# Sigmoid attention and a GELU feed-forward: weight and g tiles at their own places mod 64 bytes, and two blocks whose first products are issued in other forms

## The chip, the cores and the metric

One core of a Trainium2 chip runs the whole program. The metric is the device time of an execution in microseconds; the kernel before took 1192.64 us, the median of two runs (1191.70 and 1193.59). Its profiled execution took 1189.64 us.

## The reference

Attention with a sigmoid in place of the softmax, on 8 batches of 12 heads, 448 positions and 64 elements a head; then a feed-forward over the 3,584 tokens, of width 768 with 2,048 hidden units.

```python
scores = scale * np.matmul(q, k.transpose(0, 1, 3, 2)) - np.log(S)
attn = 1.0 / (1.0 + np.exp(-scores))
attn_out = np.matmul(attn, v)                       # 8 x 12 x 448 x 64
x = attn_out.transpose(0, 2, 1, 3).reshape(B * S, H * D)      # 3584 x 768
h = x @ w_in                                        # 3584 x 2048
g = 0.5 * h * (1.0 + erf(h / sqrt(2)))
out = g @ w_out                                     # 3584 x 768
```

The feed-forward's weights come as 64-bit floats.

## The kernel before

Attention runs first, in 24 steps of four heads each; its result x is parked in DRAM, with the model's 768 rows as 6 groups of 128 partitions and the tokens along the free dimension. Meanwhile a decoder on VectorE and ScalarE (lines 90 to 129) turns the 64-bit weights into 32-bit ones, reading every second word of `raw`, and writes them to DRAM too.

The feed-forward takes the tokens in 7 blocks of T = 512 (`t` from 0 to 6). Each block is two products. To keep precision, each operand is the sum of two rounded tiles, hi and lo (type float32r), and each product is three matmuls: lo weights by hi data, hi weights by lo data, hi weights by hi data.

- `ffn1(t)`, first product: for each of 16 units `fc` of 128 hidden rows, 6 groups `cc` of x times 3 matmuls go into one PSUM tile `ph` of 128 x 512 (lines 370 to 372). The moving operand is `xh[:, cc]` or `xl[:, cc]`, 512 words side by side. ScalarE then applies GELU twice, once to a float32 tile `gf` and once to the rounded `g` tile's first half, and VectorE subtracts the two to make the second half (lines 375 to 377).
- `ffn2(t, g)`, second product: for each of 6 groups `e` of output rows, 16 units times 3 matmuls go into `po` (lines 398 to 400); ScalarE copies `po` out, and SP's queue stores it.

So each product of a block is 288 matmuls, each with its own load of 128 x 128 weights. PSUM has four tiles for `ph` and `po` in turn.

`Weights` is what feeds the weights: `get(key)` is called as a unit begins, and `prepare_to(i + 4)` makes the units up to three ahead ready: a load from DRAM into one of three `wst` buffers (SP's queue), ScalarE's rounding to the hi part (line 184) and VectorE's subtraction for the lo part (line 185), into one of WHL = 4 `whl` buffers. The order of each engine's work is the order in which the program is written; a buffer that is asked for again waits for all who read it.

All tiles of the feed-forward have lengths that are multiples of 64 bytes, and all operands of its matmuls start a multiple of 64 bytes from their tile's start.

Of the kernel before, what the change touches and what calls it, by code (L numbers as in the profile page):

```python
# [8 lines left out]
F32 = mybir.dt.float32  # L9
F32R = mybir.dt.float32r  # L10
# [3 lines left out]
AF = mybir.ActivationFunctionType  # L14
ALU = mybir.AluOpType

P = 128
# [4 lines left out]
def tile_sigmoid_attention_gelu_ffn(  # L22
# [10 lines left out]
    nc = tc.nc  # L33
    B, NPAIR, _, S = q.shape
    NU = NPAIR // 2
    D = HALF
    NF, _, NC, _ = w_in.shape
    NO, _, NFH, _ = w_out.shape
# [3 lines left out]
    T = 512  # L42
# [5 lines left out]
    def psum(name, bufs):  # L48
        return tc.tile_pool(name=name, bufs=bufs, space=bass.MemoryType.PSUM)

    const = ctx.enter_context(tc.tile_pool(name="const", bufs=1))
    sb = ctx.enter_context(tc.tile_pool(name="sb", bufs=1))
# [3 lines left out]
    xh = const.tile([P, NPAIR, T], F32R, name="xh")  # L56
    xl = const.tile([P, NPAIR, T], F32R, name="xl")
# [4 lines left out]
    WU = max(NC, NFH) * P  # L62
    SUB_IN, SUB_OUT = NC * P, NFH * P // 2
    SUB = max(SUB_IN, SUB_OUT)
    WHL, WST = 4, 3
# [8 lines left out]
    def width(kind):  # L74
        return (NC if kind == "in" else NFH) * P
# [80 lines left out]
    dec = Decoder()  # L156
    AHEAD = 20

    class Weights:
# [17 lines left out]
        def prepare_to(self, n):  # L177
            while self.ready < min(n, len(self.units)):
                i = self.ready
                self.load_to(i + 1)  # L180
                t = self.staged.pop(i)
                w = width(self.units[i][1])
                hl = sb.tile([P, 2, WU], F32R, tag="whl", name=f"whl{i}", bufs=WHL)
                nc.scalar.copy(hl[:, 0, :w], t[:, :w])  # L184
                nc.vector.tensor_tensor(hl[:, 1, :w], t[:, :w], hl[:, 0, :w], op=ALU.subtract)  # L185
                self.split[i] = hl
                self.ready += 1
                self.load_to(i + WST)
# [6 lines left out]
    W = Weights()  # L195
# [4 lines left out]
    def load_x(t):  # L200
        nc.sync.dma_start(xl.bitcast(F32), scr_x[:, :, t * T : (t + 1) * T])

    def split_x():
        half = NPAIR // 2
        for h in slice(0, half), slice(half, NPAIR):
            nc.scalar.copy(xh[:, h], xl[:, h].bitcast(F32))
            nc.vector.tensor_tensor(xl[:, h], xl[:, h].bitcast(F32), xh[:, h], op=ALU.subtract)
# [151 lines left out]
                W.prepare_to(2)  # L359

    def feed_forward(ff, ps_f):
        def ffn1(t):
            g = []
            for fc in range(NF):
                ph = ps_f.tile([P, T], F32, tag="pf", name=f"ph{t}_{fc}")
                hl = W.get((t, "in", fc))
                for cc in range(NC):
                    wh = hl[:, 0, cc * P : (cc + 1) * P]
                    wl = hl[:, 1, cc * P : (cc + 1) * P]
                    nc.tensor.matmul(ph, wl, xh[:, cc], start=cc == 0, stop=False)  # L370
                    nc.tensor.matmul(ph, wh, xl[:, cc], start=False, stop=False)  # L371
                    nc.tensor.matmul(ph, wh, xh[:, cc], start=False, stop=cc == NC - 1)  # L372
                gt = ff.tile([P, 2, T], F32R, tag=f"g{fc}", name=f"g{t}_{fc}")
                gf = ff.tile([P, T], F32, tag="tmp", name=f"gf{t}_{fc}", bufs=3)
                nc.scalar.activation(gf, ph, AF.Gelu)  # L375
                nc.scalar.activation(gt[:, 0], ph, AF.Gelu)  # L376
                nc.vector.tensor_tensor(gt[:, 1], gf, gt[:, 0], op=ALU.subtract)  # L377
                g.append(gt)
                if t == 0:
                    dec.to(AHEAD + 10 * (fc + 1) / NF)  # L380
            return g

        def ffn2(t, g):
            for e in range(NE):
                po = ps_f.tile([P, T], F32, tag="pf", name=f"po{t}_{e}")
                for half in range(2):
                    hl = W.get((t, "out", 2 * e + half))
                    if t == 0:
                        dec.to(AHEAD + 10 + 2 * e + half + 1)
                    if e == 1 and half == 0 and t + 1 < NT:  # L390
                        load_x(t + 1)
                    if e == 2 and half == 0 and t + 1 < NT:
                        split_x()
                    for f in range(NFH):
                        fc = half * NFH + f
                        wh = hl[:, 0, f * P : (f + 1) * P]
                        wl = hl[:, 1, f * P : (f + 1) * P]
                        nc.tensor.matmul(po, wl, g[fc][:, 0], start=fc == 0, stop=False)  # L398
                        nc.tensor.matmul(po, wh, g[fc][:, 1], start=False, stop=False)  # L399
                        nc.tensor.matmul(po, wh, g[fc][:, 0], start=False, stop=fc == NF - 1)  # L400
                ob = ff.tile([P, T], F32, tag="tmp", name=f"ob{t}_{e}", bufs=3)
                nc.scalar.copy(ob, po)  # L402
                nc.sync.dma_start(out[e * P : (e + 1) * P, t * T : (t + 1) * T], ob)

        for t in range(NT):
            ffn2(t, ffn1(t))
# [6 lines left out]
    ff = ctx.enter_context(tc.tile_pool(name="ff", bufs=1))  # L413
    ps_f = ctx.enter_context(psum("ps_f", 4))
    feed_forward(ff, ps_f)


# [31 lines left out]
```

## Time and profile before

| | |
|---|---|
| median of the runs | 1192.64 us |
| profiled execution | 1189.64 us |
| its span, first to last instruction | 1187.9 us |
| TensorE busy, matmuls | 1170.8 us, 5,856 |
| granted TensorE clock | 0.999 |
| ScalarE, VectorE busy | 547.5 us, 528.1 us |
| GpSimd busy | 36.0 us |
| DMA, mean | 164 GB/s |

Attention takes about the first 267 us of the span, and the feed-forward's seven blocks the rest. In the rows of a profile an engine's time is busy time, PE is TensorE with its matmuls, PEld its weight loads, DVE VectorE, ACT ScalarE, and SPq the queue that issues DMAs. A matmul's duration includes the time until its last result is written, so matmuls that follow each other overlap in the rows; the distance from start to start is what one costs in a stream.

### The profile page before, as it was taken

What the parts mean: (1) busy time and instruction counts of PE and PEld (TensorE: products, weight loads), DVE (VectorE), ACT (ScalarE), POOL (GpSimd) and SP (SyncE); (2) the same over time, 40 slices, a digit from 0 to 9 for tenths busy, and PEclk for the clock granted to TensorE, in tenths of its full rate; (3) what the DMA queues carried; (4) which work ended last, traced back from release to release, by engine and by line L of the source; (5) the groups of instructions that cost most, each with busy time, mean ns of one, the idle gap of its engine ahead of it and who ended that gap; (6) DMA issues with size and microseconds to landing.
All of it is one profiled execution on the core that took longest, in us unless ns stands there. A gap on an engine that the chain in (4) does not pass through costs nothing.

```text
span 1187.9 us, 14649 instructions
## 1 busy us (share of the span) xinstructions
PE 1170.8 (99%) x5856; PEld 884.8 (74%) x5856; DVE 528.1 (44%) x643; ACT 547.5 (46%) x751; POOL 36.0 (3%) x56
## 2 busy tenths in 40 slices
PE   6999999999999999999999999999999999999998
PEld 3554544548888788888888888888888888888887
DVE  4777776447878334323432243324432343323420
ACT  6777777666644344324432343324432443324420
POOL 0111111000000000000000000000000000000000
PEclk9999999999999999999999999999999999999999
DMA  9999988646767533523343333433343334433330
GB/s 304 304 286 295 293 281 257 203 159 214 237 244 262 182 94 124 181 81 109 118 171 98 107 111 115 155 119 94 120 159 111 102 106 169 120 98 98 120 115 27
DMA packets 71300, 194.42 MB, mean 164 GB/s; under 512 B 6976, under 2 KB 19648, under 8 KB 71232
## 3 DMA queue, kind: packets, MB, share of 16 engines
q1 hardware_dynamic: 65536, 169.89, 45.6%
q0 software_dynamic: 5696, 23.60, 4.9%
q8 instruction: 46, 0.75, 0.3%
q14 instruction: 22, 0.18, 0.0%
HBM read 158.86 MB, written 34.60 MB: 163 GB/s over the span
## 4 chain that ended last, share of the span: by engine, by line
PE 81%; issue 15%; DMA 2%; POOL 1%; SPq 0%; ACT 0%; DVE 0%; POOLq 0%; ACTq 0%
PE po L398 11%; PE po L399 11%; PE po L400 11%; PE ph L370 11%; PE ph L371 11%; PE ph L372 11%; PE pav L298 7%; PE sc L264 5%; DMA qk<-k_dram 1%; PE sc_t L277 1%; PE pav L311 1%; POOL scr_out L128 0%; POOL scr_x L327 0%; DMA wst<-scr_out 0%; DMA scr_out<-wd_out 0%
## 5 line engine op out<-in xcount | busy, mean ns | idle before, releaser
L185 DVE TENSOR_TENSOR whl<-wst,whl 128x768 fp32r<-128x768 f32 (+1 forms) x196 | 210.0, 1072 | 299.3 <-ACT whl L184 296.5
L398 PE MATMUL po<-g,whl 128*128 128x512 f32 x672 | 261.8, 390 | 2.5 <-DVE whl L185 2.4
L370 PE MATMUL ph<-xh,whl 128*128 128x512 f32 x672 | 261.5, 389 | 0.0
L400 PE MATMUL po<-g,whl 128*128 128x512 f32 x672 | 261.4, 389 | 0.0
L399 PE MATMUL po<-g,whl 128*128 128x512 f32 x672 | 261.4, 389 | 0.0
L372 PE MATMUL ph<-xh,whl 128*128 128x512 f32 x672 | 261.4, 389 | 0.0
L371 PE MATMUL ph<-xl,whl 128*128 128x512 f32 x672 | 261.4, 389 | 0.0
L184 ACT CAST whl<-wst 128x768 fp32r<-128x768 f32 (+1 forms) x196 | 181.7, 928 | 140.5 <-PE po L400 117.2
L377 DVE TENSOR_TENSOR g<-gf,g 128x512 fp32r<-128x512 f32 x112 | 77.4, 692 | 232.0 <-ACT g L376 231.9
L375 ACT ACTIVATE gf<-ph 128x512 f32<-128x512 f32 x112 | 67.0, 598 | 224.4 <-PE ph L372 196.9
L252 ACT ACTIVATE a<-sc 128x896 f32<-128x896 f32 x144 | 121.9, 919 | 59.9 <-PE sc L264 59.9
L398 PEld LDWEIGHTS po<-g,whl 128*128 128x128 f32 x672 | 126.1, 188 | 29.9 <-DVE whl L185 3.8
L370 PEld LDWEIGHTS ph<-xh,whl 128*128 128x128 f32 x672 | 126.1, 188 | 26.9 <-DVE whl L185 0.7
L372 PEld LDWEIGHTS ph<-xh,whl 128*128 128x128 f32 x672 | 126.1, 188 | 26.3
L400 PEld LDWEIGHTS po<-g,whl 128*128 128x128 f32 x672 | 126.1, 188 | 26.3
L399 PEld LDWEIGHTS po<-g,whl 128*128 128x128 f32 x672 | 126.1, 188 | 26.1
L371 PEld LDWEIGHTS ph<-xl,whl 128*128 128x128 f32 x672 | 126.1, 188 | 26.1
L298 PE MATMUL pav<-a,v 128*64 128x448 f32 x576 | 118.6, 547 | 0.0
L402 ACT COPY ob<-po 128x512 f32<-128x512 f32 x42 | 24.7, 587 | 172.5 <-PE po L400 170.9
L298 PEld LDWEIGHTS pav<-a,v 128*64 128x64 f32 x576 | 37.2, 136 | 69.7 <-issue 69.7
L376 ACT ACTIVATE g<-ph 128x512 fp32r<-128x512 f32 x112 | 66.4, 593 | 0.0
L264 PE MATMUL sc<-lo,hi 64*128 64x448 f32 x288 | 58.4, 402 | 6.8 <-DVE lo L248 6.8
(35 smaller groups left out, 666.5 us busy)
## 6 DMA issues: line engine op xcount, KB each, us to landing
wst<-scr_in SPq DMA_DIRECT2D x112, 384.0 KB, 3.2
wst<-scr_out SPq DMA_DIRECT2D x84, 512.0 KB, 3.4
v<-v_dram SPq DMA_DIRECT2D x24, 512.0 KB, 5.2
raw<-w_in_dram SPq DMA_DIRECT2D x16, 768.0 KB, 8.0
raw<-w_out_dram SPq DMA_DIRECT2D x24, 512.0 KB, 5.1
scr_x<-x POOLq DMA_DIRECT2D x24, 448.0 KB, 6.8
xl<-scr_x SPq DMA_DIRECT2D x7, 1536.0 KB, 8.0
out_dram<-ob SPq DMA_DIRECT2D x42, 256.0 KB, 2.1
```

The source lines that it names most:

```text
L184: nc.scalar.copy(hl[:, 0, :w], t[:, :w])
L185: nc.vector.tensor_tensor(hl[:, 1, :w], t[:, :w], hl[:, 0, :w], op=ALU.subtract)
L252: nc.scalar.activation(a, sc, AF.Sigmoid, bias=NEG_LOG_S, scale=SCALE)
L264: nc.tensor.matmul(sc[:, j], ks[rows(j), 1, keys], qs[rows(j), 0], start=n == 0, stop=n == 2)
L298: nc.tensor.matmul(pav[rows(j)], vals[u][:, p, j, c], a[:, j], start=p == 0 and c == 0, stop=p == 1 and c == FULL - 1,)
L370: nc.tensor.matmul(ph, wl, xh[:, cc], start=cc == 0, stop=False)
L371: nc.tensor.matmul(ph, wh, xl[:, cc], start=False, stop=False)
L372: nc.tensor.matmul(ph, wh, xh[:, cc], start=False, stop=cc == NC - 1)
L377: nc.vector.tensor_tensor(gt[:, 1], gf, gt[:, 0], op=ALU.subtract)
L398: nc.tensor.matmul(po, wl, g[fc][:, 0], start=fc == 0, stop=False)
L399: nc.tensor.matmul(po, wh, g[fc][:, 1], start=False, stop=False)
L400: nc.tensor.matmul(po, wh, g[fc][:, 0], start=False, stop=fc == NF - 1)
```

## The change

It has five parts. `whl` and `g` tiles become 16 words longer, each under a name and buffer of its own. The data in a `whl` buffer starts 0, 4, 8 or 12 words into it, by buffer; that of `g` starts `fc` words in, 0 to 15. All blocks get this.

In block 1, units 0 to 11 take the moving operand x in another order of the 512 tokens: as rows of an `a` x `b` matrix read by columns, with `a` = lap = 2 (units 0 to 3), 32 (4 to 7) and 256 (8 to 11). Neighbours in the stream lie 256, 16 and 2 words apart. The results land in PSUM in stream order, and the two GELUs read them back with a step of lap words, so that `g` is in token order again. Units 12 to 15 of block 1 issue each matmul as two of 256 tokens.

In block 2, units 0 to 7 go two by two: for each `cc` and term, the matmul of one unit and then that of the other, into two PSUM tiles. Units 8 to 15 take the three terms in the order hi by lo, hi by hi, lo by hi.

```diff
@@ -180,7 +180,9 @@
                 self.load_to(i + 1)
                 t = self.staged.pop(i)
                 w = width(self.units[i][1])
-                hl = sb.tile([P, 2, WU], F32R, tag="whl", name=f"whl{i}", bufs=WHL)
+                hl = sb.tile([P, 2 * WU + 16], F32R, tag=f"whl{i % WHL}", name=f"whl{i}", bufs=1)
+                skip = 4 * (i % WHL)
+                hl = hl[:, skip : skip + 2 * WU].rearrange("p (x n) -> p x n", x=2)
                 nc.scalar.copy(hl[:, 0, :w], t[:, :w])
                 nc.vector.tensor_tensor(hl[:, 1, :w], t[:, :w], hl[:, 0, :w], op=ALU.subtract)
                 self.split[i] = hl
@@ -359,25 +361,62 @@
                 W.prepare_to(2)
 
     def feed_forward(ff, ps_f):
+        def whole(m):
+            return [(slice(0, P), m, slice(0, T))]
+
+        def shuffled(a):
+            return lambda m: [(slice(0, P), m.rearrange("p (a b) -> p b a", a=a), slice(0, T))]
+
+        def halves(m):
+            return [(slice(0, P), m[:, i : i + T // 2], slice(i, i + T // 2)) for i in (0, T // 2)]
+
+        def form(t, fc):
+            if t == 1 and fc < 12:
+                lap = (2, 32, 256)[fc // 4]
+                return shuffled(lap), lap
+            return (halves if t == 1 else whole), 1
+
+        def hidden(t, fcs):
+            phs = [ps_f.tile([P, T], F32, tag="pf", name=f"ph{t}_{fc}") for fc in fcs]
+            hls = [W.get((t, "in", fc)) for fc in fcs]
+            late = t == 2 and fcs[0] >= NF // 2
+            order = ((0, xl), (0, xh), (1, xh)) if late else ((1, xh), (0, xl), (0, xh))
+            split_to, lap = form(t, fcs[0])
+            for cc in range(NC):
+                for n, (x, m) in enumerate(order):
+                    for ph, hl in zip(phs, hls):
+                        w = hl[:, x, cc * P : (cc + 1) * P]
+                        for c, mv, ts in split_to(m[:, cc]):
+                            o = ph[c, ts]
+                            if lap > 1:
+                                o = o.rearrange("p (b a) -> p b a", a=lap)
+                            nc.tensor.matmul(
+                                o,
+                                w[:, c],
+                                mv,
+                                start=cc == 0 and n == 0 and ts.start == 0,
+                                stop=cc == NC - 1 and n == 2 and ts.stop == T,
+                            )
+            return [ph.rearrange("p (b a) -> p a b", a=lap) for ph in phs], {"a": lap}
+
         def ffn1(t):
             g = []
-            for fc in range(NF):
-                ph = ps_f.tile([P, T], F32, tag="pf", name=f"ph{t}_{fc}")
-                hl = W.get((t, "in", fc))
-                for cc in range(NC):
-                    wh = hl[:, 0, cc * P : (cc + 1) * P]
-                    wl = hl[:, 1, cc * P : (cc + 1) * P]
-                    nc.tensor.matmul(ph, wl, xh[:, cc], start=cc == 0, stop=False)
-                    nc.tensor.matmul(ph, wh, xl[:, cc], start=False, stop=False)
-                    nc.tensor.matmul(ph, wh, xh[:, cc], start=False, stop=cc == NC - 1)
-                gt = ff.tile([P, 2, T], F32R, tag=f"g{fc}", name=f"g{t}_{fc}")
-                gf = ff.tile([P, T], F32, tag="tmp", name=f"gf{t}_{fc}", bufs=3)
-                nc.scalar.activation(gf, ph, AF.Gelu)
-                nc.scalar.activation(gt[:, 0], ph, AF.Gelu)
-                nc.vector.tensor_tensor(gt[:, 1], gf, gt[:, 0], op=ALU.subtract)
-                g.append(gt)
+            f0 = 0
+            while f0 < NF:
+                fcs = range(f0, f0 + (2 if t == 2 and f0 < NF // 2 else 1))
+                phs, like = hidden(t, fcs)
+                for fc, ph in zip(fcs, phs):
+                    gt = ff.tile([P, 2 * T + 16], F32R, tag=f"g{fc}", name=f"g{t}_{fc}", bufs=1)
+                    gt = gt[:, fc : fc + 2 * T].rearrange("p (x n) -> p x n", x=2)
+                    gf = ff.tile([P, T], F32, tag="tmp", name=f"gf{t}_{fc}", bufs=3)
+                    gv, gh = (y.rearrange("p (a b) -> p a b", **like) for y in (gf, gt[:, 0]))
+                    nc.scalar.activation(gv, ph, AF.Gelu)
+                    nc.scalar.activation(gh, ph, AF.Gelu)
+                    nc.vector.tensor_tensor(gt[:, 1], gf, gt[:, 0], op=ALU.subtract)
+                    g.append(gt)
+                f0 = fcs[-1] + 1
                 if t == 0:
-                    dec.to(AHEAD + 10 * (fc + 1) / NF)
+                    dec.to(AHEAD + 10 * f0 / NF)
             return g
 
         def ffn2(t, g):
```

TensorE's order where block 1's unit 12 begins, before (line, operation, output<-inputs, size; `ph1_12` is the PSUM tile of block 1's unit 12, and the numbers behind names are those of buffers):

```order
L370 MATMUL ph1_12_4091<-xh_64,whl40_4005 128x512
L371 MATMUL ph1_12_4091<-xl_65,whl40_4005 128x512
L372 MATMUL ph1_12_4091<-xh_64,whl40_4005 128x512
L370 MATMUL ph1_12_4091<-xh_64,whl40_4005 128x512
L371 MATMUL ph1_12_4091<-xl_65,whl40_4005 128x512
L372 MATMUL ph1_12_4091<-xh_64,whl40_4005 128x512
```

and after, where `x2` and `x4` count rows alike that follow each other:

```order
L393 MATMUL ph1_12_4091<-xh_64,whl40_4005 128x256 x2
L393 MATMUL ph1_12_4091<-xl_65,whl40_4005 128x256 x2
L393 MATMUL ph1_12_4091<-xh_64,whl40_4005 128x256 x4
L393 MATMUL ph1_12_4091<-xl_65,whl40_4005 128x256 x2
L393 MATMUL ph1_12_4091<-xh_64,whl40_4005 128x256 x4
```

Each matmul of 512 columns has become two of 256, one behind the other; the terms follow as before. The units with a lap read like those of before in this listing, since it gives sizes and no steps.

ScalarE's order where block 2 begins, before (`whl59` is the weight unit 59, block 2's unit 3; `gf2_0` and `g2_0` are the GELUs of its unit 0):

```order
L402 COPY ob1_5_4581<-po1_5_4522 128x512
L184 CAST whl59_4585<-wst59_4526 128x768
L375 ACTIVATE gf2_0_4609<-ph2_0_4584 128x512
L376 ACTIVATE g2_0_4608<-ph2_0_4584 128x512
L184 CAST whl60_4614<-wst60_4555 128x768
L375 ACTIVATE gf2_1_4638<-ph2_1_4613 128x512
L376 ACTIVATE g2_1_4637<-ph2_1_4613 128x512
L184 CAST whl61_4643<-wst61_4588 128x768
```

and after:

```order
L441 COPY ob1_5_4653<-po1_5_4594 128x512
L186 CAST whl59_4658<-wst59_4598 128x768
L186 CAST whl60_4663<-wst60_4627 128x768
L413 ACTIVATE gf2_0_4705<-ph2_0_4656 128x512
L414 ACTIVATE g2_0_4704<-ph2_0_4656 128x512
L413 ACTIVATE gf2_1_4710<-ph2_1_4657 128x512
L414 ACTIVATE g2_1_4709<-ph2_1_4657 128x512
L186 CAST whl61_4716<-wst61_4661 128x768
L186 CAST whl62_4721<-wst62_4666 128x768
```

The cast of unit 60 has moved ahead of the first pair's GELUs. Its buffer is that of unit 56, which this pair's matmuls still read.

## The prediction

> **What bounds the kernel now.** I read the page's totals first, then the chain of waits, then the feed-forward in windows by stage, and last single matmuls in the timeline.
>
> ```profile
> span 1187.9 us, 14649 instructions
> PE 1170.8 (99%) x5856; PEld 884.8 (74%) x5856; DVE 528.1 (44%) x643; ACT 547.5 (46%) x751; POOL 36.0 (3%) x56
> PEclk9999999999999999999999999999999999999999
> PE 81%; issue 15%; DMA 2%; POOL 1%; SPq 0%; ACT 0%; DVE 0%; POOLq 0%; ACTq 0%
> PE po L398 <- DVE whl L185: 2.4, 2, 1.7
> ```
>
> TensorE is busy for 99% of the span at full granted clock, the chain that ends last is made of its matmuls, and over the whole feed-forward the matmuls of L398 waited 2.4 us for prepared weights. So an edit counts if it changes how far apart the matmuls start, or makes one of them wait. A window per stage shows the distance. The rows are the first product (ffn1) and the second (ffn2) of block 1, then ffn1 of block 2; the columns are window, length, and busy time with counts of PE, PEld, DVE, ACT, POOL.
>
> ```profile
> 400.76:466.04 65.28, 65.28 (x290) 54.05 (x289) 26.51 (x31) 29.09 (x47) 0.00 (x0) 1.00 0.36 111
> 466.04:531.32 65.28, 65.28 (x290) 54.05 (x289) 18.02 (x15) 18.13 (x21) 0.00 (x0) 1.00 0.41 131
> 531.32:596.60 65.28, 65.28 (x290) 54.05 (x289) 26.52 (x31) 29.07 (x47) 0.00 (x0) 1.00 0.34 111
> ```
>
> Each product is 16 x 18 = 288 matmuls (the counts take in two at the edges): 65.28 / 288 = 226.7 ns from start to start, in both products alike. Single rows say the same, and that each matmul's own weight load (PEld) starts with the matmul before it and so lies under it:
>
> ```profile
> 449.94 0.39 PE L371 MATMUL ph<-xl,whl 128*128 128x512 f32 x1
> 449.95 0.19 PEld L372 LDWEIGHTS ph<-xh,whl 128*128 128x128 f32 x1
> 450.17 0.39 PE L372 MATMUL ph<-xh,whl 128*128 128x512 f32 x1
> 450.17 0.19 PEld L370 LDWEIGHTS ph<-xh,whl 128*128 128x128 f32 x1
> 450.40 0.39 PE L370 MATMUL ph<-xh,whl 128*128 128x512 f32 x1
> ```
>
> Of the 226.7 ns, how much goes with the columns? The scores have 448 columns instead of 512 and come in pairs on two halves of the array:
>
> ```profile
> 61.43 0.19 PEld L264 LDWEIGHTS sc<-lo,hi 64*128 64x128 f32 x2 [0.70 <-ACT me L113]
> 61.54 0.19 PEld L264 LDWEIGHTS sc<-hi,lo 64*128 64x128 f32 x2
> 61.74 0.36 PE L264 MATMUL sc<-hi,lo 64*128 64x448 f32 x2
> 61.94 0.37 PE L264 MATMUL sc<-hi 64*128 64x448 f32 x2
> ```
>
> They stand 0.20 us apart, 0.027 less for 64 columns fewer: 0.42 ns a column, and so 226.7 - 512 x 0.417 = 13 ns that every matmul pays whatever its width. The two loads at the top, with nothing before them, start 0.11 us apart; that is how fast loads can follow each other.
>
> **The change part by part.**
>
> *Strided x (block 1, 12 of 16 units, 216 matmuls).* The moving operand's elements are taken 256 words apart (lap 2), 16 apart (lap 32) and 2 apart (lap 256), 72 matmuls each. PSUM is still written in order. No matmul of the trace reads with a step, so the price needs bounds. Below it is nothing: 226.7 ns stays. For what a matmul costs when each column takes twice as long to come, the nearest row is the probability times value product, which streams plain 32-bit floats at the same granted clock (the same run of matmuls, its first 4 and its first 6, that is one pair of 448 columns more):
>
> ```profile
> 63.45 0.97 PE L298 MATMUL pav<-a,v 128*64 128x448 f32 x4
> 63.45 1.35 PE L298 MATMUL pav<-a,v 128*64 128x448 f32 x6
> ```
>
> 0.38 us for 448 columns is 0.85 ns a column, 434 ns for 512, and 207 ns over the present spacing. Which laps pay it? One row of the trace reads SBUF with a step, the weight decoder, which takes every second word of `raw`; beside it a VectorE cast of contiguous data:
>
> ```profile
> L100 DVE TENSOR_SCALAR me<-raw 128x512 uint32<-128x512 uint32 x24 | 10.1, 421 | 0.0
> L100 DVE TENSOR_SCALAR me<-raw 128x768 uint32<-128x768 uint32 x16 | 9.0, 562 | 0.0
> L247 DVE CAST hi<-qk 128x896 fp32r<-128x896 f32 x24 | 15.2, 633 | 0.4 <-DMA qk<-k_dram 0.4
> ```
>
> 256 elements more cost 141 ns, 0.55 ns each, and at that slope 896 would take 421 + 384 x 0.55 = 632 ns, which is what the contiguous cast takes. A step of two words costs VectorE nothing. I take that for lap 256, and the doubled stream for laps 2 and 32, where no two neighbours in the stream are near each other in memory: 144 x 207 = 29.8 us. The ends are 0 and all three laps doubled, 216 x 207 = 44.7 us; a dearer case is a rival. That the far steps pay at all is my choice, and the weakest point here.
>
> The Trainium skill's page "SBUF — State Buffer", in section "Door 1: The DMA port swizzle", says that SBUF is read in lines of 16 bytes and that two hits on a line are needed for full bandwidth. By that rule lap 256 (two words of each line) is free and the other two pay; it gives no price, and the decoder's row agrees with it for the step of two.
>
> *Halves (block 1, last 4 units).* 72 matmuls become 144 of 256 columns, each with its own weight load. By the columns' slope a half takes 256 x 0.417 + 13 = 120 ns, over the 0.11 us in which loads can follow each other, so loads stay covered and a pair costs 240 for 227: 72 x 13 = 1.0 us. If the loads didn't fit, a half couldn't cost more than a whole does now: 72 x 227 = 16.3 us at most. From below, nothing: no row shows a matmul without the 13 ns.
>
> *Two by two, and the other order (block 2).* 288 matmuls of the same shape, each with its load: 0. Before, too, hi weights are loaded twice in a row (L371, L372), and each load has its own row. What moves is on ScalarE and VectorE:
>
> ```profile
> L375 ACT ACTIVATE gf<-ph 128x512 f32<-128x512 f32 x112 | 67.0, 598 | 224.4 <-PE ph L372 196.9 <-issue 27.6
> L376 ACT ACTIVATE g<-ph 128x512 fp32r<-128x512 f32 x112 | 66.4, 593 | 0.0
> L184 ACT CAST whl<-wst 128x768 fp32r<-128x768 f32 x112 | 93.4, 836 | 52.6 <-PE po L400 40.1 <-DMA wst<-scr_in 12.5
> L185 DVE TENSOR_TENSOR whl<-wst,whl 128x768 fp32r<-128x768 f32 x112 | 107.2, 957 | 98.3 <-ACT whl L184 96.2
> ```
>
> A pair asks for the weights four units on, whose buffer is that of the pair's first unit, so this cast now waits for the pair's own matmuls, and the pair's four gelus queue behind it on ScalarE. After a pair ends ScalarE runs cast, four gelus, cast: 0.84 + 2 x (0.60 + 0.59) + 0.84 = 4.1 us, and with VectorE's 0.96 the second weight of the pair after next is ready 5.0 us on. TensorE needs it after one more pair, 36 x 0.227 = 8.2 us. Cover left: 3.2 us. The gelus have emptied the pair's two PSUM buffers 3.2 us after its end, against the same 8.2. VectorE's queue (subtraction of weights, then two of g) follows within it, and the loads on SP's queue stand as far ahead as before. If the cover went, each of four pairs would lose what is over.
>
> *Gelu with a step in PSUM (block 1).* ScalarE is busy 29.09 of 65.28 us in this stage, by the window above. Were all 24 gelus twice as long, 24 x 0.6 = 14 us more still fit. 0.
>
> *Places mod 64 bytes.* Every one of the 4,032 feed-forward matmuls has another place for its weights, and those of ffn2 for g too (one word further per unit). No row shows an operand off a multiple of 64 bytes. From below: the 13 ns goes everywhere, -4,032 x 13 = -52 us. From above: the eight g tiles on odd words stream like the probabilities, 1,008 x 207 = +209 us. In each tile the words still follow each other, as they do in all contiguous rows, so I take 0 and keep both ends as rivals.
>
> **Sum**: 29.8 + 1.0 = 30.8 us. The profiled execution took 1189.64 us, 1.7 over its span; it becomes 1220.4. The median before is 1192.64, 3.0 above that execution, so the forecast is 1223.4, and its own range goes from 1222 (halves at nothing) to 1239 (halves at their most).
>
> **The rivals.** 2% of 1192.64 is 24 us, about what a measurement of this kernel can tell from no change.
>
> 1. *The step is free.* TensorE takes 32-bit words from any place at 0.44 ns each. For it: the step of two words is free on VectorE, and no row shows a stall by an address. Against it: the fixed 13 ns and the slower 0.85 ns rows show a stream that isn't far from some limit. Time: 1192.6 + 1.0 = 1193.6; ends not slower. It decides if laps 2 and 32 together cost under 23 us, 160 ns a matmul.
> 2. *All three laps double*: 44.7 + 1.0, 1238.3. For it: any step breaks a pair of neighbours; against it, the decoder's row.
> 3. *The read unit holds four words.* With one word used of it, a column takes four times 0.417: 853 + 13 = 866 ns, 640 over the present. Laps 2 and 32 then cost 92.2, lap 256 (two words of four, doubled) 14.9, halves 1.0: 1300.7. If lap 2, which goes back and forth between two places, keeps both units at hand, 46.1 less: 1254.6. For it: 4 bytes in 0.42 ns is the fastest stream of any row here (VectorE's is 0.55 ns, ScalarE's 128x768 cast 1.09), so spare reads are unlikely. Against it: nothing in the trace measures such a step.
>  The Trainium skill's "Vector Engine (DVE) Microarchitecture Reference", section "Measured stream behaviour on trn2", has 1.73 ns a column against 1.054 when one VectorE source hops every element, and the full rate for a source that alternates between two regions. An estimate from that page, 512 x 1.73 = 886 ns, would put the far laps beside rival 3, with lap 2 free or not; no run here shows it yet.
> 4. *One lap alone pays* (the 64-byte step, say): 14.9 + 1.0, 1208.5, within 2%.
> 5. *The places help.* The 13 ns is weight loads and streams that meet because all tiles start on the same 64 bytes; apart, they don't. With the step free it gives 1193.6 - 52 = 1141; with the forecast's laps 1171. For it: the 13 ns is there in every row, with a load under each matmul. Against it: it is the same to 0.1 ns in stages with other operands.
> 6. *Odd words hurt*: the 209 us above, about 1400 or more.
>
> **How the numbers follow.** Forecast 0.26; rival 1, 0.24; rival 2, 0.17; rival 3, 0.20 (0.11 for 1301, 0.09 for 1255); rival 4, 0.07; rival 5, 0.04; rival 6, 0.02. Slower by over 2%: 0.26 + 0.17 + 0.20 + 0.02 = 0.65. Within 2%: 0.24 + 0.07 = 0.31. Faster: 0.04. The range reaches from 1190.5 (rival 1 with halves at nothing and the runs' own spread) to 1260 (rival 3 with lap 2 free): it leaves out 1301, rivals 5 and 6, 0.17 in all.
>
> **What would show it.** In the profile after, ffn1 of block 1 should last 65.3 + 30.8 = 96 us, with matmuls 434 ns apart in its first eight units, 227 in the next four, and 120 in the halves; ffn1 of block 2 and every ffn2 should last 65.28, with no wait of TensorE for weights in block 2. The forecast is wrong if the first four or the second four units keep 227 ns or go past 434, if the third four leave 227, or if the window of any other block has another length than 65.28 us: then the places mod 64 bytes matter.

## The result, and the profile after

The changed kernel takes 1240.16 us, the median of two runs (1239.88 and 1240.45), against 1192.64: 47.5 us more, a ratio of 1.0403 with a 95% interval of 1.0382 to 1.0424. It is slower, as forecast, by half as much again as the 30.8 us of the sum, and inside the range.

The page's span, totals, clock and chain, after, and then the row of TensorE's waits for weights:

```profile
span 1238.1 us, 14800 instructions
PE 1220.5 (99%) x5928; PEld 893.9 (72%) x5928; DVE 528.0 (43%) x643; ACT 547.2 (44%) x751; POOL 36.2 (3%) x56
PEclk8999999999999999999999999999999999999999
PE 82%; issue 14%; DMA 2%; POOL 1%; SPq 0%; ACT 0%; DVE 0%; POOLq 0%; ACTq 0%
```

```profile
PE po L437 <- DVE whl L187: 1.3, 2, 1.1
```

TensorE is as full as before and waits no longer for weights (1.3 us against 2.4), so the time went into the spacing of matmuls. Windows by form show where. The first four rows are block 1's first product: laps 2, 32 and 256 with 72 matmuls each, then the halves with 144. The next two are block 2's first and second product, the last is block 3's first product, which has no form of its own, only the new places.

```profile
404.60:420.13 15.53, 15.53 (x73) 13.61 (x72) 5.92 (x7) 6.73 (x11) 0.00 (x0) 1.00 0.39 126
420.13:451.32 31.19, 31.19 (x74) 14.81 (x72) 6.61 (x8) 7.23 (x12) 0.00 (x0) 1.00 0.20 63
451.32:483.95 32.63, 32.63 (x73) 14.97 (x72) 6.61 (x8) 7.23 (x12) 0.00 (x0) 1.00 0.18 57
483.95:501.20 17.25, 17.25 (x145) 17.24 (x144) 7.41 (x8) 7.87 (x12) 0.00 (x0) 1.00 0.28 93
568.23:634.60 66.37, 66.37 (x289) 54.08 (x288) 26.55 (x31) 28.70 (x47) 0.00 (x0) 1.00 0.35 109
634.60:701.59 66.99, 66.99 (x289) 54.35 (x288) 18.02 (x15) 18.11 (x21) 0.00 (x0) 1.00 0.39 128
701.59:767.79 66.20, 66.20 (x289) 54.06 (x288) 26.54 (x31) 29.10 (x47) 0.00 (x0) 1.00 0.35 110
```

Before, 72 matmuls took 72 x 226.7 ns = 16.32 us, and each product 65.28 us. So:

| | us now | us before | per matmul | difference |
|---|---|---|---|---|
| lap 2 | 15.53 | 16.32 | 216 ns | -0.8 |
| lap 32 | 31.19 | 16.32 | 433 ns | +14.9 |
| lap 256 | 32.63 | 16.32 | 453 ns | +16.3 |
| halves | 17.25 | 16.32 | 120 ns a half | +0.9 |
| a plain first product | 66.20 | 65.28 | 230 ns | +0.9 each |
| block 2's first product | 66.37 | 65.28 | 230 ns | +1.1 |
| a second product | 66.99 | 65.28 | 233 ns | +1.7 each |

Block 1's forms cost 31.3 us together, near the sum of the prediction, but not by its terms: lap 2 is *faster* than neighbouring words, and lap 256, taken as free, is the dearest. The rest is in every block, and so belongs to the places.

### The profile page after: what moved, and what is told of

The parts are those of the page before. It is cut to its first block, busy times and chain, and to the rows that moved or that the text cites. A ratio compares the mean times of both kernels' runs of the same rounds, so it can differ in the third digit from the quotient of the medians.

```text
span 1238.1 us, 14800 instructions
## 1 busy us (share of the span) xinstructions
PE 1220.5 (99%) x5928; PEld 893.9 (72%) x5928; DVE 528.0 (43%) x643; ACT 547.2 (44%) x751; POOL 36.2 (3%) x56
## 4 chain that ended last, share of the span: by engine, by line
PE 82%; issue 14%; DMA 2%; POOL 1%; SPq 0%; ACT 0%; DVE 0%; POOLq 0%; ACTq 0%
PE ph L393 35%; PE po L437 11%; PE po L439 11%; PE po L438 11%; PE pav L300 6%; PE sc L266 5%; DMA qk<-k_dram 2%; PE sc_t L279 1%; PE pav L313 1%; POOL scr_out L128 0%; POOL scr_x L329 0%; DMA wst<-scr_out 0%; DMA scr_out<-wd_out 0%; SPq L226 0%; SPq L223 0%
## 5 line engine op out<-in xcount | busy, mean ns | idle before, releaser
L393 PE MATMUL ph<-xh,whl 128*128 128x512 f32 (+1 forms) x1392 | 436.2, 400 | 0.0
L393 PEld LDWEIGHTS ph<-xh,whl 128*128 128x128 f32 x1392 | 258.5, 189 | 73.8 <-issue 22.9
L393 PE MATMUL ph<-xl,whl 128*128 128x512 f32 (+1 forms) x696 | 271.1, 401 | 0.0
L437 PE MATMUL po<-g,whl 128*128 128x512 f32 x672 | 265.7, 395 | 1.3 <-DVE whl L187 1.3
L439 PE MATMUL po<-g,whl 128*128 128x512 f32 x672 | 264.9, 394 | 0.0
L438 PE MATMUL po<-g,whl 128*128 128x512 f32 x672 | 264.8, 394 | 0.0
L393 PEld LDWEIGHTS ph<-xl,whl 128*128 128x128 f32 x696 | 130.0, 189 | 35.9 <-issue 11.1
L437 PEld LDWEIGHTS po<-g,whl 128*128 128x128 f32 x672 | 126.3, 188 | 30.8 <-DVE whl L187 2.1
L250 DVE TENSOR_TENSOR lo<-qk,hi 128x896 fp32r<-128x896 f32 x48 | 52.5, 1093 | 26.1 <-ACT hi L247 24.2
L326 DVE COPY x<-pav 128x448 f32<-128x448 f32 x48 | 29.9, 624 | 72.8 <-PE pav L300 41.9
```

The source lines that it names most:

```text
L393: nc.tensor.matmul(o, w[:, c], mv, start=cc == 0 and n == 0 and ts.start == 0, stop=cc == NC - 1 and n == 2 and ts.stop == T,)
```

## The experiments

Each experiment starts from the kernel before, unless it is said otherwise. The theories in the expectations bear letters; the same letter can stand for different things in different runs, and each expectation says what it means by it. Two of them last: the stream of moving words has a price by its order alone; and the places of weights and moving data, relative to each other, add something.

### The places alone

```diff
-hl = sb.tile([P, 2, WU], F32R, tag="whl", name=f"whl{i}", bufs=WHL)
+hl = sb.tile([P, 2 * WU + 16], F32R, tag=f"whl{i % WHL}", name=f"whl{i}", bufs=1)
+skip = 4 * (i % WHL)
+hl = hl[:, skip : skip + 2 * WU].rearrange("p (x n) -> p x n", x=2)
-gt = ff.tile([P, 2, T], F32R, tag=f"g{fc}", name=f"g{t}_{fc}")
+gt = ff.tile([P, 2 * T + 16], F32R, tag=f"g{fc}", name=f"g{t}_{fc}", bufs=1)
+gt = gt[:, fc : fc + 2 * T].rearrange("p (x n) -> p x n", x=2)
```

> The changed kernel's places alone (weights and g as in the change), all matmuls in the form of before. From the changed kernel's trace: first products 66.2 us instead of 65.3 in each block, second products 67.0 instead of 65.3: 7 x 0.9 + 6 x 1.7 = 16.5 us, 1209 us, with block 0's second product limited by the weights' arrival anyway. If the places cost only in company with the other forms: 1193 us.

1209.51 us against 1193.27 for the kernel before beside it: a ratio of 1.0133 (1.0119 to 1.0146), 16.2 us. That is under 2%, but clear of the spread of the runs (1208.8 to 1210.0 against 1191.0 to 1194.9). Its windows for block 1's first and second product:

```profile
404.19:470.39 66.20, 66.20 (x289) 54.08 (x288) 26.54 (x31) 29.05 (x47) 0.00 (x0) 1.00 0.33 110
470.39:537.38 66.99, 66.99 (x289) 54.41 (x288) 18.03 (x15) 18.10 (x21) 0.00 (x0) 1.00 0.38 128
```

These are the changed kernel's 66.20 and 66.99, and 1209 us was expected. The forms of blocks 1 and 2 are what is left: in the changed kernel block 1's first product takes 96.60 us (the sum of its four windows) against 66.20 here, 30.4 us more, and block 2's 0.2 us more, while the medians of the two kernels differ by 30.7 us. So the account closes to a microsecond: 16.2 + 30.4 + 0.2 = 46.8 of the 47.5 us. (The 31.3 us of the table count from the old places, and so hold the 0.9 us that the places cost block 1's first product.)

### The weights' place swept, with x at its old place and 32 bytes on

```diff
-hl = sb.tile([P, 2, WU], F32R, tag="whl", name=f"whl{i}", bufs=WHL)
+hl = sb.tile([P, 2 * WU + 128], F32R, tag=f"whl{i % WHL}", name=f"whl{i}", bufs=1)
+t_, kind_, u_ = self.units[i]
+skip = u_ if t_ % 2 == 0 and kind_ == "in" else 4 * u_
+hl = hl[:, skip : skip + 2 * WU].rearrange("p (x n) -> p x n", x=2)
```

> All matmuls in the form of before, x and g at their old places; only the weights' place moves: in odd blocks unit fc of the first product starts 16*fc bytes into its buffer (0 to 240), in even blocks 4*fc bytes; the second product's units 16 bytes apart. Theory M (a weight load and the moving stream under way meet in SBUF, by their places mod 64): spacings in the odd blocks' first products repeat with period 4, as in the changed kernel: 227, 232, 233, 227 ns; in even blocks something between 227 and 234; lap 2 not used, so nothing falls below 226. Theory A (an operand off a 64-byte start costs by itself): every unit but those at 0, 64, 128 and 192 bytes is dearer by about the same 4 to 6 ns. Whole time by both about 1200 to 1210 us.

1213.5 us in one run. Windows of 18 matmuls in block 1, where the weights go on by 16 bytes from unit to unit: units 0, 1, 4 and 15, with weights 0, 16, 64 and 240 bytes on; then in block 2, where they go on by 4 bytes: units 1, 2, 4 and 7, with weights 4, 8, 16 and 28 bytes on.

```profile
406.64:410.74 4.10, 4.10 (x19) 3.38 (x18) 0.96 (x1) 1.32 (x2) 0.00 (x0) 1.00 0.63 197
410.74:414.83 4.09, 4.09 (x19) 3.38 (x18) 1.65 (x2) 1.80 (x3) 0.00 (x0) 1.00 0.29 90
423.22:427.41 4.19, 4.19 (x19) 3.38 (x18) 1.65 (x2) 1.81 (x3) 0.00 (x0) 1.00 0.33 95
469.24:473.32 4.08, 4.08 (x19) 3.38 (x18) 1.92 (x2) 2.02 (x3) 0.00 (x0) 1.00 0.37 131
544.18:548.37 4.19, 4.19 (x19) 3.38 (x18) 1.65 (x2) 1.80 (x3) 0.00 (x0) 1.00 0.32 106
548.37:552.53 4.16, 4.16 (x20) 3.38 (x19) 1.66 (x2) 1.81 (x3) 0.00 (x0) 1.00 0.29 92
556.73:560.93 4.20, 4.20 (x20) 3.40 (x19) 1.65 (x2) 1.81 (x3) 0.00 (x0) 1.00 0.30 95
569.29:573.51 4.22, 4.22 (x19) 3.38 (x18) 1.65 (x2) 1.81 (x3) 0.00 (x0) 1.00 0.29 93
```

Divided by 18: 228, 227, 233 and 227 ns; then 233, 231, 233 and 234. Both theories are wrong in part. A start off 64 bytes isn't dear by itself, since 16 and 240 bytes on cost nothing in block 1; and there is no period of 64 bytes, since 64 bytes on costs what 4 do. Nor does the number of bytes on decide alone: 16 bytes on costs nothing in block 1's unit 1, and 6 ns in block 2's unit 4. The two have different weight buffers (these start 8,704 bytes apart here), different PSUM tiles, and different units before them, one at 0 and one at 12 bytes. No place got below 226.6 ns. (In the changed kernel each buffer is 64 bytes longer than 8,192, so that with the skips its four really lie 0, 80, 160 and 240 bytes further on, not 0 to 48.)

Then x was moved as well:

```diff
-xh = const.tile([P, NPAIR, T], F32R, name="xh")
-xl = const.tile([P, NPAIR, T], F32R, name="xl")
+XS = 8
+xs_ = const.tile([P, 2 * NPAIR * T + 128], F32R, name="xs_")
+xh, xl = (
+    xs_[:, XS + i * NPAIR * T : XS + (i + 1) * NPAIR * T].rearrange("p (c t) -> p c t", c=NPAIR)
+    for i in range(2)
+)
```

To make room, the attention has one buffer fewer for its probabilities (`bufs=10` instead of 11). A first version (`e2_w_sweep_x8`), with `xh` and `xl` lengthened each by itself and all 11 buffers, has no result: its tiles need more of SBUF than there is. The one tile for x is 512 bytes longer than the two before, so the weights' buffers, which lie behind it, have all moved by 512 bytes too.

> The sweep of the weights' places once more, with x (xh and xl) 8 words, 32 bytes, further on; one buffer fewer for the probabilities in the attention makes room. In the sweep without it the odd blocks' first products read, for units 0 to 15 (weights 0, 16, 32 ... 240 bytes on): 227, 227, 233, 233, 233, 232, 234, 233, 234, 233, 233, 230, 229, 233, 233, 227 ns. Theory R (only the places of the two operands relative to each other count): the same row moved on by two units, with 233, 227, 227, 227, 233 at units 0 to 4. Theory A (each operand's own place counts): the low units stay at 0, 1 and 15, or all rise. The second products, with g at its old place, read as in the first sweep.

1209.7 us in one run. Block 2's windows for units 9, 10, 12 and 15 here, with weights 36, 40, 48 and 60 bytes on, that is 4, 8, 16 and 28 beyond x, in the same four buffers as units 1, 2, 4 and 7 above, and then block 1's for unit 3, 48 bytes on, that is 16 beyond x:

```profile
574.42:578.61 4.19, 4.19 (x20) 3.38 (x18) 1.65 (x2) 1.80 (x3) 0.00 (x0) 1.00 0.34 99
578.61:582.76 4.15, 4.15 (x19) 3.38 (x18) 1.65 (x2) 1.81 (x3) 0.00 (x0) 1.00 0.25 89
586.97:591.16 4.19, 4.19 (x19) 3.40 (x18) 1.65 (x2) 1.81 (x3) 0.00 (x0) 1.00 0.30 114
599.52:603.75 4.23, 4.23 (x20) 3.38 (x19) 1.92 (x2) 2.02 (x3) 0.00 (x0) 1.00 0.35 124
416.12:420.21 4.09, 4.09 (x20) 3.38 (x18) 1.65 (x2) 1.81 (x3) 0.00 (x0) 1.00 0.31 99
```

233, 231, 233 and 235 ns: the row has moved with x by 32 bytes, to within 0.01 us a window, so of the two operands' places it is the distance that counts (theory R), and 512 bytes more of it change nothing. Block 1's row moves by two units in the same way, as expected, though that gives each step another buffer: unit 3 has 227 ns, as unit 1 had.

The riddle of 16 bytes stays: again it is cheap in block 1, behind a unit at 0, and dear in block 2's unit 12, behind a unit at 12. A longer period of the distance is no likely answer. From unit 1 of the first kernel, cheap, to unit 12 of this one, dear, the distance changes by 8,704 - 512 = 8,192 bytes, so no power of two up to that can be the period. That at such a distance a unit keeps the spacing which the one before it left is a rival that fits, but no run tells it from an effect of the buffer or of the PSUM tile. The kernel before has equal places everywhere, and no other was cheaper: the places could only lose, and they are not what lap 2 gains by.

### Is it the load that the stream loses 11 ns to?

Here the 13 ns of the prediction are called 11 ns, the part that lap 2 saves (226.7 - 215.8). Two kernels add, in block 1, each unit's 18 matmuls once more, into a PSUM tile `pd` that nobody reads, with another load: with fewer columns of weights, and with weights taken some words apart.

```diff
+if t == 1:
+    w = 128 - 32 * (fc // 4)
+    pd = ps_f.tile([P, T], F32, tag="pf", name=f"pd{t}_{fc}")
+    for cc in range(NC):
+        wh = hl[:, 0, cc * P : cc * P + w]
+        wl = hl[:, 1, cc * P : cc * P + w]
+        nc.tensor.matmul(pd[:w], wl, xh[:, cc], start=cc == 0, stop=False)
+        nc.tensor.matmul(pd[:w], wh, xl[:, cc], start=False, stop=False)
+        nc.tensor.matmul(pd[:w], wh, xh[:, cc], start=False, stop=cc == NC - 1)
```

> The kernel before, and in block 1 each unit's 18 matmuls once more into a PSUM tile that nobody reads, with 128 weight columns (units 0 to 3), 96, 64 and 32 (units 12 to 15). The stream of 512 words is the same, only the load under it gets shorter. Theory M (the 13 ns over 512 columns is the meeting of stream and load): 227, 224, 221 and 218 ns for these added matmuls. Rival F (a contiguous stream at this rate pays it whatever is loaded): 227 ns in all of them. Whole time about 1192.6 + 288 x 0.22 = 1257 us.

1261.3 us in one run. Windows of the added matmuls of units 1, 5, 9 and 13 (PE and PEld alone):

```profile
418.35:422.43 4.08, 4.08 (x18) 3.19 (x17) 1.00 0.09 33
451.09:455.24 4.15, 4.15 (x18) 2.75 (x17) 1.00 0.07 22
484.09:488.23 4.14, 4.14 (x18) 2.28 (x17) 1.00 0.05 18
517.00:521.17 4.17, 4.17 (x18) 1.85 (x17) 1.00 0.25 93
```

227, 231, 230 and 232 ns: the load's busy time falls from 3.19 to 1.85 us, and the spacing rises a little, where theory M had it fall to 218. The second kernel replaces the `w` columns by 128 of them `s` words apart, with `s` = 0, 2, 4, 6 (0 repeats one column); `...` stands for lines as above:

```diff
+if t == 1:
+    s = (0, 2, 4, 6)[fc // 4]
+    def walk(m):
+        if s == 0:
+            return m[:, 0:1].to_broadcast([P, P])
+        return m[:, : s * P].rearrange("p (b a) -> p a b", a=s)[:, 0]
...
+        wh = walk(hl[:, 0])
+        wl = walk(hl[:, 1])
+        nc.tensor.matmul(pd, wl, xh[:, cc], start=cc == 0, stop=False)
...
```

> The kernel before, and in block 1 each unit's 18 matmuls once more into a PSUM tile that nobody reads, with 128 weights taken 0, 2, 4 and 6 words apart (four units each), all from the start of the unit's weights; the moving stream of 512 words side by side is as before. In the run with fewer weight columns the spacing didn't fall (226.6, 230, 230 and 231.6 ns for 128, 96, 64 and 32). Theory M2 (the way the load goes through SBUF decides what the stream loses): with step 0, which stays at one place, about 216 ns or another value well away from 227, and different values for steps 2, 4, 6. Rival F (a stream of neighbouring words loses about 11 ns by itself, and the load's place adds 0 to 7): 227 to 234 for all four.

1259.6 us in one run. The added matmuls of units 1, 5, 9 and 13 again:

```profile
415.26:419.42 4.16, 4.16 (x18) 3.19 (x17) 1.00 0.07 24
448.27:452.47 4.20, 4.20 (x18) 3.28 (x17) 1.00 0.07 26
481.46:485.69 4.23, 4.22 (x18) 4.08 (x18) 1.00 0.05 18
514.86:519.13 4.27, 4.27 (x18) 4.11 (x18) 1.00 0.24 92
```

231, 233, 235 and 237 ns. A load that stays at one place doesn't free the stream either. So the load theory falls for these 11 ns: a stream of neighbouring words paid them under each of the eight loads tried (rival F, of both runs), and 0 to 11 ns more came on top. F had up to 234 in the second run; the 235 and 237 may be the load itself, since with words 4 and 6 apart one load lasts 0.31 us in the trace, longer than the spacing, against 0.19 with neighbours. Whether the 11 ns would be there with no load at all isn't shown, since each matmul here brings its own.

### Which orders of the stream are dear

Old places throughout. Block 1: laps 2, 4, 8, 16, 64, 128, 256 and 1, two units each. Block 2: runs of `c` neighbouring words, hopping over `a` places. The matmuls use `o`, `mh` and `ml`, and the GELUs read back as in the change; `...` stands for those lines.

```diff
+a, c = form(t, fc)
+y = dict(a=a, c=c)
+o = ph.rearrange("p (b a c) -> p b a c", **y) if a > 1 else ph
...
+    mh, ml = xh[:, cc], xl[:, cc]
+    if a > 1:
+        mh, ml = (m.rearrange("p (a b c) -> p b a c", **y) for m in (mh, ml))
...
```

> Old places of all tiles. Block 1: two units each with lap 2, 4, 8, 16, 64, 128, 256, 1. Block 2: runs of c neighbouring words, hopping between a places: (a,c) = (2,2), (2,4), (2,16), (32,2), (32,4), (32,8), (4,2), (4,4). Theory P (SBUF gives pairs of words: two neighbours per read, and the two latest reads are kept): lap 2 216 ns; laps 4 and 8 to 256 about 432 to 453; every run of two words or more 216 to 227. Rival Q (16-byte units, with four of them kept): laps 2 and 4 216, and runs of two words over 32 places 432, runs of four 216 to 227. Whole time by P about 1192.6 + 12 units x 18 x 0.21 = 1238 us.

1256.7 us in one run. Block 1's windows for laps 2, 4, 8, 16 and 256, of 36 matmuls each, then block 2's for (a, c) = (2, 2), (2, 4), (32, 2) and (32, 4):

```profile
403.08:410.85 7.77, 7.77 (x37) 6.80 (x36) 2.61 (x3) 3.12 (x5) 0.00 (x0) 1.00 0.49 154
410.85:421.05 10.20, 10.20 (x38) 6.91 (x37) 3.30 (x4) 3.61 (x6) 0.00 (x0) 1.00 0.34 108
421.05:438.65 17.60, 17.60 (x38) 7.49 (x37) 3.31 (x4) 3.66 (x6) 0.00 (x0) 1.00 0.15 50
438.65:454.25 15.60, 15.60 (x37) 7.38 (x36) 3.31 (x4) 3.63 (x6) 0.00 (x0) 1.00 0.17 50
486.33:502.57 16.24, 16.24 (x37) 7.45 (x36) 3.57 (x4) 3.82 (x6) 0.00 (x0) 1.00 0.18 65
576.05:588.27 12.22, 12.22 (x37) 7.10 (x36) 2.61 (x3) 3.14 (x5) 0.00 (x0) 1.00 0.36 119
588.27:597.28 9.01, 9.01 (x37) 6.81 (x36) 3.30 (x4) 3.71 (x6) 0.00 (x0) 1.00 0.18 49
605.93:621.44 15.51, 15.51 (x38) 7.38 (x36) 3.30 (x4) 3.61 (x6) 0.00 (x0) 1.00 0.23 73
621.44:629.59 8.15, 8.15 (x38) 6.77 (x37) 3.30 (x4) 3.61 (x6) 0.00 (x0) 1.00 0.18 52
```

Lap 2 stands at 216 ns with the old places too, so the new places cost it nothing in the changed kernel; lap 4 at 283, lap 8 at 489, lap 16 at 433, lap 256 at 451. Over 32 places, runs of two words cost 431 ns and runs of four 226. So theory P (pairs) falls and its rival Q fits in the unit: runs of four words, 16 bytes, have the full rate over 32 places, and runs of two take about twice the time. But single words take no longer than pairs (433 against 431), so it isn't a fixed price for each unit read. Q's four kept units are wrong, since lap 4 already pays. No theory had the runs between two places: single words 216, pairs 340, fours 250. That stays open, as does why lap 8 is dearer than lap 16.

Lap 2 was then tried over shorter distances, within parts of the 512 tokens, from 256 words down to 2 (`n`, the number of parts, is the `a` that the lines below take):

```diff
+n = 1 << (fc // 2) if t == 1 else 0
...
+y = dict(h=a, a=2)
+o = ph.rearrange("p (h b a) -> p h b a", **y) if a else ph
...
+        mh, ml = (m.rearrange("p (h a b) -> p h b a", **y) for m in (mh, ml))
...
```

> Old places, only block 1's first product differs: the stream goes back and forth between two places, as with lap 2, but within parts of the 512 tokens, so that the two places lie 256, 128, 64, 32, 16, 8, 4 and 2 words apart (units 0 and 1, 2 and 3, and so on). Theory K (two reads of 16 bytes are kept, wherever they lie): 216 ns at every distance down to 4 words, and at 2 words, where both places lie in the same 16 bytes, near 227. Rival D (the distance of 1 KB matters): 216 at 256 words, from 283, the figure of lap 4 at 128 words, upwards for others.

1189.0 us in one run. The windows of units 0 to 13 (252 matmuls, 256 to 4 words) and of units 14 and 15 (36 matmuls, 2 words):

```profile
402.81:457.20 54.39, 54.39 (x254) 47.62 (x252) 22.69 (x27) 25.02 (x41) 0.00 (x0) 1.00 0.35 114
457.20:465.39 8.19, 8.19 (x37) 6.76 (x36) 3.83 (x4) 4.04 (x6) 0.00 (x0) 1.00 0.39 129
```

215.8 ns at every distance down to 4 words, 227.5 at 2. That is what theory K said: turns of single words between two units of 16 bytes spare the 11 ns, and the distance doesn't count (rival D falls). That two such units are *kept* is not shown by it: by K pairs between two places, which find the same two units again, should be as cheap, and they took 340 ns. So the order's price is measured, and the mechanism behind it stays open.

### Lap 2 everywhere

The order that the change had in 4 of its 16 units of one block, for every matmul of the feed-forward, with all tiles at their old places:

```diff
+def lap(m):       return m.rearrange("p (a b) -> p b a", a=2)
+def straight(o):  return o.rearrange("p (b a) -> p b a", a=2)
+def back(o):      return o.rearrange("p (b a) -> p a b", a=2)
+def halved(m):    return m.rearrange("p (a b) -> p a b", a=2)
-nc.tensor.matmul(ph, wl, xh[:, cc], start=cc == 0, stop=False)
+nc.tensor.matmul(straight(ph), wl, lap(xh[:, cc]), start=cc == 0, stop=False)
-nc.scalar.activation(gf, ph, AF.Gelu)
+nc.scalar.activation(halved(gf), back(ph), AF.Gelu)
...
```

> Lap 2 for every matmul of the feed-forward, in both products and all blocks, with all tiles at their old places; PSUM is read back with a step of two words. Theory M (with lap 2 the stream no longer loses the 11 ns to the weight load under it): 227 falls to 215.6 ns in both products, 4,032 x 11.1 = 45 us, 1148 us. Rival (the 216 ns of the changed kernel's lap-2 units came from the weights' new places or holds for x alone): 1170 us if only the first products gain, 1193 if none does. A rival on the other side: the last copies out of PSUM or GELUs with a step become late and take part of it back.

1155.54 us, a ratio of 0.9689 (0.9673 to 0.9705): 37 us saved of 45. The windows of block 1's two products, of block 0's second, and of eight matmuls in it; then the same product in the kernel before, and TensorE's row of waits for weights:

```profile
402.48:464.64 62.16, 62.16 (x289) 54.43 (x288) 26.57 (x32) 29.05 (x47) 0.00 (x0) 1.00 0.35 118
464.64:526.80 62.16, 62.16 (x289) 54.43 (x288) 17.92 (x15) 18.09 (x21) 0.00 (x0) 1.00 0.40 138
329.26:402.48 73.22, 64.91 (x289) 55.31 (x288) 54.08 (x73) 32.12 (x44) 3.98 (x6) 0.98 0.68 236
375.09:378.60 3.51, 3.51 (x8) 2.82 (x9) 3.14 (x6) 1.74 (x3) 0.00 (x0) 0.51 0.49 159
```

```profile
332.05:400.76 68.71, 66.19 (x290) 53.82 (x289) 47.97 (x69) 31.26 (x43) 3.20 (x6) 1.00 0.72 245
```

```profile
PE po L412 <- DVE whl L185: 8.3, 4, 4.2
```

62.16 / 288 = 215.8 ns in both products, the number of theory M (its cause, the load, has fallen above, in runs made after this one). The gain that is missing went into block 0, where the faster stream runs into the weight decoder: 73.22 us against 62.16, 11.1 too many, where the kernel before had 68.71 against 65.28, 3.4 too many. 8.3 of the 11.1 us are waits for weights. Most of the others come behind the longest wait, 4.2 us: there eight matmuls took 3.51 us, twice the usual, with a granted clock of 0.51. So the last kernel decodes three more pieces during the attention, and takes lap 2 to the scores too:

```diff
-AHEAD = 20
+AHEAD = 23
-sc[:, j], ks[rows(j), 1, keys], qs[rows(j), 0], start=n == 0, stop=n == 2
+straight(sc[:, j]), ks[rows(j), 1, keys], lap(qs[rows(j), 0]), start=n == 0, stop=n == 2
...
```

> Lap 2 in both products of the feed-forward and in the scores, and three more pieces of the weight decoder during the attention (23 instead of 20). With lap 2 in the feed-forward alone it was 1155.5 us, 8.3 us of it waits of block 0's second product for decoded weights. Theory M: the 432 pairs of score matmuls go from 203 to about 191 ns, 5 us, and most of the 8 us wait goes: 1143 us. Rival: the attention is not limited by its matmuls' spacing (VectorE and ScalarE are three quarters busy there, and now get more to do), so nothing or less than nothing comes of it: 1150 to 1160 us.

1141.87 us, a ratio of 0.9564 (0.9550 to 0.9578), 51 us under the kernel before. The window of block 0's second product, and then two pairs of score matmuls from the timeline:

```profile
328.27:391.07 62.80, 62.42 (x289) 54.44 (x288) 44.55 (x58) 28.15 (x38) 3.23 (x5) 1.00 0.67 237
```

```profile
64.60 0.35 PE L280 MATMUL sc<-hi 64*128 64x448 f32 x2
64.79 0.35 PE L280 MATMUL sc<-lo,hi 64*128 64x448 f32 x2
```

The wait is gone: 73.22 to 62.80 us, 10.4 of the 11.4 us between the spans of the two profiled executions (1152.2 and 1140.8 us). Pairs of scores stand 0.19 us apart instead of 0.20, but of the 5 us that theory M forecast for them little came: the feed-forward's first matmul starts at 264.94 us instead of 266.32, 1.4 us earlier. The attention also decodes three more pieces here, and what each of the two did to it wasn't measured apart.

## Why the prediction was right or wrong

**Direction, bound and range: right.** TensorE's spacing set the time; no wait took its place. 1240.16 lies in the range. By the signs that the prediction itself named, though, the forecast was wrong twice: the third four units left 227 ns, and other blocks' windows left 65.28 us.

**The 1223.4 us: 17 us short, by the term for the places.** The step that failed is "In each tile the words still follow each other, as they do in all contiguous rows, so I take 0": it measured 16.2 us. What counts is not whether words follow each other but how far the weights lie from the moving data; rival 5 had the two meeting where their places are equal, and that turned out to be as cheap as any.

**Lap 32: right in size**, 14.9 us forecast and 14.9 measured, 433 ns against 434 from the plain 32-bit product's row. Nothing shows that the two have one cause: the price is not a plain doubling for all far steps, since lap 8 takes 489 ns.

**Lap 2: wrong in sign**, 14.9 forecast, -0.8 measured. The step that failed was that no two neighbours in the stream lie near each other in memory, and so it doubles. The runs show that neighbours in the stream may lie far apart when it takes turns between two places, and that this order spares even the 11 ns that ordinary streams pay; by what mechanism stays open. I had read those 13 ns as a fixed cost of every matmul, and "no row shows a matmul without the 13 ns" was true only of the rows at hand. The Trainium skill's "Vector Engine (DVE) Microarchitecture Reference", section "Measured stream behaviour on trn2", says of VectorE that a source alternating between two regions keeps the full rate; this trace shows no loss for TensorE either, with 216 ns. Rival 3 had a way for lap 2 to be spared, but not to gain.

**Lap 256: wrong**, 0 forecast, 16.3 measured. The step "A step of two words costs VectorE nothing. I take that for lap 256" carried a row of one engine to another that takes words faster (0.42 ns each against 0.55). The rule of the Trainium skill's "SBUF — State Buffer", section "Door 1: The DMA port swizzle", two hits on a line of 16 bytes for full bandwidth, agreed with me, and the runs differ from it for this stream: with two of four words used it takes 451 ns at the old places, with four of four 226. With the two errors of opposite sign, the three laps came to 30.4 us against 29.8, which is luck and not understanding. Rival 2 has nearly the right time, 1238.3, for the wrong reasons.

**Halves: right**, 1.0 forecast (72 x 13 ns is rather 0.94) and 0.9 us measured; 120 ns a half as worked out. The rows of the scores, 0.20 us to the hundredth, were too coarse for a slope of 0.417; the halves bear it out. From 226.7 ns at 512 columns and 119.8 at 256 it is 0.418 ns a column and 13 ns a matmul, so neighbouring words do pay the 13 ns once per matmul, and only another order showed that it can be spared. **Two by two and the other order: right**: block 2's first product is 0.2 us longer than block 3's, and no wait for weights appears. **GELU with a step: right**; the mean of the first GELU over units 0 to 11 of block 1, which read with steps of 2, 32 and 256 words, is 598 ns, as before:

```profile
L413 ACT ACTIVATE gf<-ph 128x512 f32<-128x512 f32 x12 | 7.2, 598 | 58.2 <-PE ph L393 54.0 <-issue 4.2
```

**Rival 3** (four words a read) had a unit that fits the runs, and the price wrong: 433 and not 866 ns.

## What to carry to other kernels

Where TensorE is full, divide a stage by its matmuls and ask of every nanosecond over the columns what it is for: here 11 of 227 ns went with the order of the moving words, and taking tokens in turns from two places, with PSUM read back by a step, gave 4.4% on a kernel that looked finished, once the weights came early enough. Don't carry a row about steps from one engine to another, and when a sum comes out right, check its terms: two of these were wrong in opposite ways.

## What the runs showed that was not expected

- A float32r stream that takes turns between two places, 4 to 256 words apart, runs at 215.8 ns for 512 columns; neighbouring words take 226.7. Turns between two places in pairs or fours of words are slower again (340 and 250 ns).
- The distance between the weights' and the moving data's places moves the spacing between 227 and 235 ns, by steps as small as 4 bytes, with no period of 64 bytes; equal places are at the lower end. The distance alone doesn't settle it: 16 bytes cost nothing behind a unit at 0 and 6 ns behind a unit at 12, twice over, and why isn't shown.
- Fewer weight columns, or one column again and again, make the spacing no shorter (227 to 232 and 231 ns).
- Behind a wait of 4.2 us, eight matmuls of the faster kernel had half the granted clock (0.51) and took 3.51 us instead of 1.7.
